# Attention and a mixture of experts in one kernel: when weights are split, on which engine, and how many output buffers

## The chip, the cores and the metric

The kernel runs on one core of a Trainium2 chip. The metric is the device time of one execution in microseconds (us), less is better. The engines are named as the profile names them: PE is TensorE's matmuls and PEld its weight loads, DVE is VectorE, ACT is ScalarE, POOL is GpSimd, SP is SyncE, whose queue here does nothing but start transfers. "Indirect" transfers, which gather or scatter rows by a table of indices, are started by POOL.

## The reference

```python
# attention: B, H, S, D = 4, 8, 768, 64; 4 sink tokens, window 128
scores = scale * q @ k.T
scores = where(is_sink | in_window, scores, -1e9)
a = softmax(scores);  attn = a @ v
# mixture of experts: x is 3072 x 512, E = 8 experts, F = 1024
x = attn.transpose(0, 2, 1, 3).reshape(3072, 512)
e_idx = argmax(x @ w_gate);  gate_w = softmax(x @ w_gate)[e_idx]
eom = sigmoid(x @ w_output_gate)
for e in range(8):
    h = maximum(x[e_idx == e] @ w1[e], 0)           # 512 -> 1024
    out[e_idx == e] = gate_w * eom[:, e] * (h @ w2[e])   # 1024 -> 512
```

## The kernel before

Attention runs in 16 steps up to about 196 us. Its rows go to `xd` in DRAM, and a router is worked out beside it: which token goes to which expert, and tables of indices (`final_table`, the last and longest part, runs on VectorE into the time of the experts; its lines are L398 to L446).

The experts' work is cut into **slots**, numbered by k from 0 to 16 (slot 16 runs only if its table has rows, and it has none in this profile). A slot is one expert with one to three blocks of up to 256 rows, or a "half" slot of one block of fewer rows (k = 5, 9 and 13). Slots 0 to 3 are the early ones (`NE` = 4), of experts that are known before all rows are. Each slot has two products: `first`, rows by w1 (the matmul of L561, L586 or L692), with ReLU behind it, and `second`, by w2 (L671, L596 or L708).

How a slot goes, engine by engine:

- **Rows.** `gather` (L514) starts an indirect transfer on POOL, `xg` from `xd`. TensorE transposes `xg` (L532), ScalarE casts the result to `xh` (L534), VectorE makes the rest, `xl` = x − `xh` (L535). The products of all slots but 0, 1 and the half ones are made of three terms, high × high, high × low and low × high.
- **Weights.** Each product takes four chunks of 512 KB. In half slots and slots 0 and 1 a chunk is loaded straight into its place. Elsewhere it goes into one of four `raw` buffers (`RAW` = 4, L491, on SP's queue); a **split** then casts it on ScalarE to its high half (L501) and subtracts that on VectorE or POOL to get the low half (L502): POOL for the chunks 0 and 2 of a product, VectorE for 1 and 3. The places of the chunks are named a0 to a3, b0 to b2, c0 to c5; `c3h` and `c3l` are the halves in place c3.
- **Between the products.** ScalarE makes `hh` from the first product (ReLU and cast, L541), VectorE the rest `hl` (L542).
- **Outputs.** `put` scales a result into `y` on ScalarE (L652), and POOL starts an indirect transfer of it into `out` (L653). Before the change `y` has two buffers. Transfers into `out` follow each other: each one waits on a semaphore of the one before.

Nothing is scheduled by the compiler: every engine runs its instructions in the order in which the program writes them. That order comes from a **planner** inside the kernel. It walks through TensorE's steps, adding up a nominal cost in `now` (`lane_step`); after each step `supply` may write the next chunk's split (`place`) into the order, if the chunk's place has been free for `LAG` units, its load was started `LAND` = 5 units ago, and the chunk before was placed at least `PACE` ago. `place` writes the split, which frees a raw buffer by its end, and `feed` starts the next raw load. At a product's beginning `ensure` writes all chunks of it that are still missing. A unit of `now` is meant as a microsecond of TensorE's work.

The lines that decide it, before:

```python
x = items[n_put[0]]
at = free.get(x["name"], 0)
if (x["again"] or at is not None and at <= now[0] - LAG) and now[0] >= put_at[0] + PACE:
    if x["split"] is None or x.get("at", now[0]) <= now[0] - LAND:
        place()
```

Of the kernel before, what the change touches and what calls it, by code (L numbers as in the profile page):

```python
# [7 lines left out]
F32 = mybir.dt.float32  # L8
F32R = mybir.dt.float32r
BF16 = mybir.dt.bfloat16  # L10
I32 = mybir.dt.int32
# [7 lines left out]
P = 128  # L19
# [4 lines left out]
DM = H * D  # L24
E, FF = 8, 1024
ND, NF = DM // P, FF // P
KW = T * (P + 4)
XW = DM + 1
# [6 lines left out]
NE = sum(n for _, n in ROUNDS)  # L35
# [6 lines left out]
HN = U * max(SIZES)  # L42
NJ = 16
JMAX = 27
NJP = NJ + 8
# [2 lines left out]
NB, RAW = 6, 4  # L48
JOINT = ((0,), (1,), (2,), (3,))
CW = P + 4  # L50
LAG, PACE, LAND = 0.7, 1.7, 5.0


def moe_kernel(tc, qT, kx, vx, vs, wgo, w1, w2, nsink, window, out):
# [5 lines left out]
    nc = tc.nc  # L60
    ctx = ExitStack()
    with ctx:
# [5 lines left out]
        mx = ctx.enter_context(tc.tile_pool(name="mx", bufs=2))  # L68
# [216 lines left out]
        def ids_of(tabv, shape, name):  # L285

            x1 = sm.tile(shape, F32, name=name + "_x")
            nc.vector.scalar_tensor_tensor(out=x1, in0=tabv[1], scalar=128.0, in1=tabv[0], op0=ALU.mult, op1=ALU.add)
            vd = sm.tile(shape, F32, name=name + "_v")
            ts(out=vd, in0=tabv[1], scalar1=0.0, scalar2=None, op0=ALU.is_gt)  # L290
            idm = sm.tile(shape, F32, name=name)
            nc.vector.scalar_tensor_tensor(out=idm, in0=x1, scalar=1.0 - P, in1=vd, op0=ALU.add, op1=ALU.mult)
            return idm
# [75 lines left out]
        def final_table(mp):  # L369
# [12 lines left out]
            yield "B"  # L382

            idm = ids_of((tab[:, 0], tab[:, 1]), [P, E, NJ], "idm")
            every = mp.tile([P, E, NJP, 4], I32, name="every", bufs=1)
            nc.vector.memset(every[:, :, NJ:NJP, 0:1], 0)
            for c, pad in ((1, NTOK), (2, 2 * NTOK), (3, 2 * NTOK)):
                nc.vector.memset(every[:, :, NJ:NJP, c:c + 1], pad)
# [2 lines left out]
            p = sm.tile([P, E, NJ], F32, name="pads_all", bufs=1)  # L391
# [7 lines left out]
            key = sm.tile([P, E], F32, name="key")  # L399
# [60 lines left out]
        w1v = w1.rearrange("e (d p) f -> e p d f", p=P)  # L460
        w2v = w2.rearrange("e (f p) d -> e p f d", p=P)

        def load_weights(which, ereg, slot, whole=False, parts=False):


            loads, splits = [], []
            src, k, n = ((w1v, ND, FF), (w2v, NF, DM))[which]
            his, los = [], []
            kk = k // 4
            for i in range(4):  # L470
                view = src[bass.ds(ereg, 1), :, i * kk:(i + 1) * kk, :].rearrange("o p k n -> p (o k) n")
                if whole:
                    if i % 2 == 0:
                        pool, name = slot()

                    def straight(pool=pool, name=name, i=i, view=view):
                        hi = (pool or pools[name[0]]).tile([P, kk, n], F32, name=name + "hl"[i % 2])
                        nc.sync.dma_start(out=hi, in_=view)
                        his.extend(hi[:, j, :] for j in range(kk))

                    if parts:
                        loads.append(straight)
                    else:
                        straight()
                    continue
                pool, name = slot()
                raws = []

                def load(view=view, raws=raws):
                    raws.append(stg.tile([P, kk, n], F32, name="raw"))  # L490
                    nc.sync.dma_start(out=raws[0], in_=view)  # L491

                def cast(pool=pool, name=name):
                    hi, lo = ((pool or pools[name[0]]).tile([P, kk, n], F32R, name=name + x) for x in "hl")
                    his.extend(hi[:, j, :] for j in range(kk))
                    los.extend(lo[:, j, :] for j in range(kk))
                    return hi, lo

                def split(raws=raws, cast=cast, eng=nc.vector if i % 2 else nc.gpsimd):
                    hi, lo = cast()  # L500
                    nc.scalar.copy(out=hi, in_=raws[0])  # L501
                    eng.tensor_tensor(out=lo, in0=raws[0], in1=hi.bitcast(F32), op=ALU.subtract)  # L502

                if parts:
                    loads.append(load)
                    splits.append(split)
                else:
                    load()
                    split()
            return ((his, los), loads, splits) if parts else (his, los)  # L510

        def gather(mp, ids, n=NTOK):
            xg = mp.tile([P, XW], F32, name="xg", bufs=3)
            nc.gpsimd.indirect_dma_start(out=xg, out_offset=None, in_=xd[0:n + 1, :],  # L514
                                         in_offset=bass.IndirectOffsetOnAxis(ap=ids[0], axis=0))
            return xg, mp.tile([P, 1], F32, name="sc", bufs=6)
# [131 lines left out]
            return hs  # L648

        def put(mp, ys, sc, m, where, rows, ids):  # L650
            y = mp.tile([P, DM], F32, name="y", bufs=2)[:, 0:m]
            nc.scalar.activation(out=y, in_=ys[:, 0:m], func=AF.Copy, scale=sc)  # L652
            nc.gpsimd.indirect_dma_start(out=where, out_offset=bass.IndirectOffsetOnAxis(ap=ids, axis=0),  # L653
                                         in_=y, in_offset=None, bounds_check=rows - 1, oob_is_err=False)
# [59 lines left out]
        def expert_reg(ap):  # L714
            return nc.sync.value_load(ap, min_val=0, max_val=E - 1)


        plan = [(order_i[0:1, r:r + 1], [(idx_e[:, 0, r, j:j + 1], idx_e[:, 1, r, j:j + 1]) for j in range(2)], False) for r in range(NE)]
# [4 lines left out]
        steps = []  # L723
# [26 lines left out]
        ws = {}  # L750
# [5 lines left out]
        def slot():  # L756
            name = next(order)
            return pools.get(name[0]), name

        with ExitStack() as actx:  # L760
# [220 lines left out]
            items, raws, names, free = [], [], {(0, 0): aa[:2], (0, 1): aa[2:], (1, 0): bb[:2], (1, 1): bb[2:] + aa[:1]}, {}  # L981
            for x in aa + bb:
                free[x] = None
            now, put_at, n_put, n_raw = [0.0], [0.0], [0], [0, 0]

            def build():
                if not todo or todo[0][0] >= NE and later:
                    return False
                k, w = todo.pop(0)
                if "e%d" % k not in ws:  # L990
                    ws["e%d" % k] = expert_reg(plan[k][0])
                used = names[k, w] = []

                def named():
                    pool, name = slot()
                    used.append(name)
                    return pool, name

                half = plan[k][2]
                ws[k, w], loads, splits = load_weights(w, ws["e%d" % k], named, half, True)  # L1000
                for i in range(4):
                    x = dict(key=(k, w), name=used[i // 2 if half else i], again=half and i % 2 == 1, load=loads[i],
                             split=None if half else splits[i])
                    items.append(x)
                    if not half:
                        raws.append(x)
                return True

            def feed():

                while n_raw[0] < n_raw[1] + RAW:
                    if n_raw[0] == len(raws):
                        if not build():
                            return
                        continue
                    x = raws[n_raw[0]]
                    x["load"]()
                    x["at"] = now[0]
                    n_raw[0] += 1

            def place():
                x = items[n_put[0]]
                n_put[0] += 1
                assert x["again"] or free.get(x["name"], 0) is not None
                free[x["name"]] = None
                if x["split"] is None:
                    x["load"]()
                else:
                    if "at" not in x:
                        feed()  # L1030
                    x["split"]()
                    n_raw[1] += 1
                    feed()
                put_at[0] = now[0]

            def supply():
                if n_put[0] == len(items) and not build():
                    return
                x = items[n_put[0]]
                at = free.get(x["name"], 0)  # L1040
                if (x["again"] or at is not None and at <= now[0] - LAG) and now[0] >= put_at[0] + PACE:
                    if x["split"] is None or x.get("at", now[0]) <= now[0] - LAND:
                        place()

            def ensure(key):
                while not all(x["key"] != key for x in items[n_put[0]:]) or key in todo:
# [224 lines left out]
            with tc.manual_schedule(engines={ET.PE, ET.Activation, ET.DVE, ET.Pool, ET.SP}):  # L1271
                for i in range(NP + 2):
                    if i == NP:
                        qctx.close()
                        mp = mctx.enter_context(tc.tile_pool(name="mp", bufs=2, side="right", reuse_waits="tile"))
# [196 lines left out]
```

## Time and profile before

| | |
|---|---|
| time before, median of 3 runs | 614.37 us (611.58 to 616.38) |
| the profiled execution's own time | 610.17 us |
| its span, first to last instruction | 608.4 us |
| mean granted TensorE clock | 0.952 of full |
| busy: PE, PEld | 521.0 us (86%), 393.6 us (65%) |
| busy: DVE, ACT, POOL | 325.5 us (54%), 269.0 us (44%), 302.4 us (50%) |
| DMA | 112.84 MB, 185 GB/s on average |

The profile describes one execution. Busy shares are averages over stages of quite different kinds, so the prediction looks at stretches of the span. In a row of the timeline the columns are the start and the length in us, the engine, the line, the operation, the output and inputs with their shapes, and, in brackets, how long the engine was idle just before and what ended that. A row ending in x4 groups four like instructions. The granted clock is the share of full speed at which TensorE was let run in a stretch; 0.50 is half speed. The last matmul ends at about 596 us; the last transfer into `out` takes the rest.

### The profile page before, as it was taken

To read this page: it belongs to the slowest core of one execution; us is meant where nothing else is said; L and a number is where in the kernel's file an instruction comes from. 1 tells how busy PE (TensorE), PEld (TensorE's weight loads), DVE (VectorE), ACT (ScalarE), POOL (GpSimd) and SP (SyncE) were. 2 spreads that over 40 slices of the span, in tenths; PEclk is the share of its full clock that TensorE was granted. 3 is DMA by queue.
4 is the path that set the end of the run, shared out by engine and by line. 5 is a ranking of instruction groups with operands and counts; after the bars stand their busy time and mean duration, and the time that the engine had idled before them with its cause. 6 is when DMAs were issued, how large, how long until landed. Compare 5 with 4: busy or idle time off the path is not lost. (4 is left out here: it accounts for less than half of the span.)

```text
span 608.4 us, 10491 instructions
## 1 busy us (share of the span) xinstructions
PE 521.0 (86%) x3432; PEld 393.6 (65%) x3432; DVE 325.5 (54%) x734; ACT 269.0 (44%) x721; POOL 302.4 (50%) x330
## 2 busy tenths in 40 slices
PE   3999999998799989399999989987999967958961
PEld 1566666665467638159989669866778757638740
DVE  5576798787686689942423642422335342342560
ACT  2577656666553225232633452433345451343420
POOL 4567667756763335424343755343347463353440
PEclk9999999999999999789999999998999987987976
DMA  6166865678987973454576666383836739464590
GB/s 217 59 154 176 188 124 134 191 139 183 265 144 218 203 216 107 149 164 141 172 260 224 226 229 210 122 272 120 296 114 209 242 126 343 156 236 148 143 378 22
DMA packets 72497, 112.84 MB, mean 185 GB/s; under 512 B 12044, under 2 KB 38672, under 8 KB 72434
## 3 DMA queue, kind: packets, MB, share of 16 engines
q1 hardware_dynamic: 67970, 98.16, 56.3%
q0 software_dynamic: 4464, 13.91, 6.3%
q8 instruction: 30, 0.49, 0.4%
q14 instruction: 33, 0.27, 0.1%
HBM read 98.28 MB, written 13.45 MB: 184 GB/s over the span
## 5 line engine op out<-in xcount | busy, mean ns | idle before, releaser
L831 ACT ACTIVATE e<-s,nmx 128x132 f32<-128x132 f32 x192 | 69.5, 367 | 66.5 <-DVE nmx L829 59.0
L819 PE MATMUL s<-kr,qr 64*128 64x260 f32 (+1 forms) x384 | 63.4, 431 | 17.1 <-ACT e L831 11.4
L542 DVE SCALAR_TENSOR_TENSOR hl<-s,hh 128x512 fp32r<-128x512 f32 (+1 forms) x32 | 24.2, 758 | 76.4 <-ACT hh L541 73.4
L819 PEld LDWEIGHTS s<-kr,qr 64*128 64x128 f32 x384 | 30.2, 198 | 41.3 <-ACT e L831 30.1
L541 ACT ACTIVATE hh<-s 128x512 fp32r<-128x512 f32 (+1 forms) x32 | 20.9, 652 | 75.2 <-PE s L561 70.8
L653 POOL DMA_INDIRECT out_dram<-y,idx x20 | 25.1, 1256 | 48.7 <-ACT y L652 23.0
L829 DVE TENSOR_REDUCE nmx<-s 128x2 f32<-128x264 f32 x96 | 41.5, 432 | 3.3
L806 POOL TENSOR_SCALAR qr<-qr 128x256 f32<-128x256 f32 x48 | 39.9, 851 | 1.6 <-DMA qr<-in_qT_dram 1.6
L535 DVE TENSOR_TENSOR xl<-tp,xh 128x512 fp32r<-128x512 f32 x21 | 14.4, 690 | 48.1 <-ACT xh L534 48.1
L84 POOL TENSOR_SCALAR_AFFINE_SELECT g<-f 128x512 f32<-128x512 f32 (+1 forms) x48 | 28.3, 590 | 21.0 <-DVE f L848 18.4
L831 ACT ACTIVATION_READ_ACCUMULATOR e<-s,nmx 128x1 f32 x192 | 37.7, 196 | 0.0
L825 DVE COPY_PREDICATED s<-maskf,s 128x256 f32<-128x256 int32 x80 | 33.7, 421 | 6.6 <-PE s L819 6.4
L532 PE MATMUL tp<-ident,xg 128*128 128x128 f32 x84 | 14.2, 296 | 20.9 <-DMA xg<-xd,idx_e 11.8
L534 ACT CAST xh<-tp 128x512 fp32r<-128x512 f32 x21 | 12.3, 587 | 41.2 <-PE tp L532 41.2
L842 PE MATMUL tp<-ident,e 128*128 128x128 f32 x192 | 29.3, 291 | 0.1
L842 PEld LDWEIGHTS tp<-ident,e 128*128 128x128 f32 x192 | 21.4, 146 | 11.4 <-issue 5.7
L84 POOL TENSOR_SCALAR_AFFINE_SELECT f<-f 128x512 f32<-128x512 f32 (+1 forms) x48 | 27.1, 564 | 3.3
L532 PEld LDWEIGHTS tp<-ident,xg 128*128 128x128 f32 x84 | 10.9, 151 | 25.8 <-DMA xg<-xd,idx_e 12.6
L514 POOL DMA_INDIRECT xg<-xd,idx x21 | 24.6, 1173 | 5.9 <-issue 4.0
L889 PE MATMUL oA<-f,vt 128*64 128x128 f32 x256 | 26.5, 285 | 0.4 <-DVE hl L871 0.2
L502 POOL TENSOR_TENSOR c0l<-raw,c0h 128x1024 fp32r<-128x1024 f32 x4 | 9.7, 2430 | 23.7 <-ACT c0h L501 23.7
L652 ACT ACTIVATE y<-oA,sc 128x512 f32<-128x512 f32 (+1 forms) x16 | 10.4, 650 | 23.4 <-DMA out_dram<-y,idx 9.3
(652 smaller groups left out, 1614.8 us busy)
## 6 DMA issues: line engine op xcount, KB each, us to landing
raw<-in_w_dram SPq DMA_DIRECT2D x88, 512.0 KB
kr<-in_kx_dram SPq DMA_DIRECT2D x16, 396.0 KB
qr<-in_qT_dram SPq DMA_DIRECT2D x16, 384.0 KB
vt<-in_vx_dram SPq DMA_DIRECT2D x16, 384.0 KB
xd<-x SPq DMA_DIRECT2D x16, 384.0 KB
a0h<-in_w_dram SPq DMA_DIRECT2D x4, 512.0 KB
a0l<-in_w_dram SPq DMA_DIRECT2D x4, 512.0 KB
b0h<-in_w_dram SPq DMA_DIRECT2D x3, 512.0 KB
```

The source lines that it names most:

```text
L84: nc.gpsimd.affine_select(out=ap, in_=ap if src is None else src, pattern=pattern, compare_op=op, fill=fill, base=base, channel_multiplier=cm)
L514: nc.gpsimd.indirect_dma_start(out=xg, out_offset=None, in_=xd[0:n + 1, :], in_offset=bass.IndirectOffsetOnAxis(ap=ids[0], axis=0))
L532: nc.tensor.transpose(out=tp[:, d, :], in_=xg[:, d * P:(d + 1) * P], identity=ident)
L542: nc.vector.scalar_tensor_tensor(out=lo, in0=ps, scalar=0.0, in1=hi.bitcast(F32), op0=ALU.max, op1=ALU.subtract)
L653: nc.gpsimd.indirect_dma_start(out=where, out_offset=bass.IndirectOffsetOnAxis(ap=ids, axis=0), in_=y, in_offset=None, bounds_check=rows - ...
L806: nc.gpsimd.tensor_scalar(out=q, in0=q, scalar1=SCALE, scalar2=None, op0=ALU.mult)
L819: nc.tensor.matmul(out=s[:, a, o0:P + CW], lhsT=z["q"][r, t * P:(t + 1) * P], rhs=z["k"][r, k0:k0 + P + CW - o0], start=True, stop=True)
L825: nc.vector.copy_predicated(out=both[:, :, 4:CW], mask=bc(maski[:, 1, 4:CW], 1, 2), data=s[:, :, 0:P])
L829: nc.vector.tensor_reduce(out=m, in_=both, axis=AX.X, op=ALU.max, negate=True)
L831: nc.scalar.activation(out=z["e"][:, t, a, :], in_=both[:, a, :], func=AF.Exp, bias=m[:, a:a + 1], scale=1.0, accum_out=z["rs"][:, t, a:a ...
L842: nc.tensor.transpose(out=tp[:, k, :], in_=z["e"][:, 2 * j + k // 2, k % 2, 4:CW], identity=ident)
L889: nc.tensor.matmul(out=o, lhsT=v[:, kt, r], rhs=src[:, kt, a, :], start=t == kt == 0 or t == kt + 1 == 4, stop=False, skip_group_check=True)
```

## The change

1. The pace at which splits are written is no longer 1.7 units throughout. The planner works out when each product begins (`due`, from 3.6 units for a half slot's product and 5.6 per block for others). A chunk whose product begins within 20 units (`SOON`) is placed 1.3 units after the last, one with more time 3.0 units after it.
2. The straight loads of half slots no longer count for the pace, and up to two places are looked at after each step.
3. From slot 4 on, POOL makes the low half of chunk 2 alone; VectorE makes the other three. Over the program 18 splits move from POOL (44 before, 26 now) to VectorE (44 before, 62 now).
4. `y` has four buffers (`YB`). To make room, a table of `final_table` (`every`) is put into the buffer that `xl` uses later.

```diff
-LAG, PACE, LAND = 0.7, 1.7, 5.0
+YB, XB = 4, 3
+LAG, PACE, SOON, LAND = 0.7, (3.0, 1.3), 20.0, 5.0
...
-            every = mp.tile([P, E, NJP, 4], I32, name="every", bufs=1)
+            every = mx.tile([P, ND, HN], F32R, name="xl", bufs=1).bitcast(I32).rearrange("p d c -> p (d c)")
+            every = every[:, 0:E * NJP * 4].rearrange("p (e j c) -> p e j c", e=E, j=NJP)
...
-                def split(raws=raws, cast=cast, eng=nc.vector if i % 2 else nc.gpsimd):
+                def split(raws=raws, cast=cast, eng=nc.gpsimd if i in onpool else nc.vector):
...
-            y = mp.tile([P, DM], F32, name="y", bufs=2)[:, 0:m]
+            y = mp.tile([P, DM], F32, name="y", bufs=YB)[:, 0:m]
...
+            due, t = {}, 4 * NF * 1.75
+            for f, k in steps + [("first", len(plan) - 1), ("second", len(plan) - 1)]:
+                due[k, 0 if f == "first" else 1] = t
+                t += 3.6 if plan[k][2] else 5.6 * len(plan[k][1])
...
-                ws[k, w], loads, splits = load_weights(w, ws["e%d" % k], named, half, True)
+                ws[k, w], loads, splits = load_weights(w, ws["e%d" % k], named, half, True, (0, 2) if k < NE else (2,))
...
-                put_at[0] = now[0]
 
             def supply():
-                if n_put[0] == len(items) and not build():
+                for _ in range(2):
+                    if n_put[0] == len(items) and not build():
+                        return
+                    x = items[n_put[0]]
+                    at = free.get(x["name"], 0)
+                    if not x["again"] and (at is None or at > now[0] - LAG):
+                        return
+                    if x["split"] is None:
+                        place()
+                        continue
+                    if now[0] >= put_at[0] + PACE[due[x["key"]] < now[0] + SOON] and x.get("at", now[0]) <= now[0] - LAND:
+                        place()
+                        put_at[0] = now[0]
                     return
```

TensorE's instructions stand in the same order before and after; those of ScalarE, VectorE, POOL and SP move. In the changed kernel the lines above are 1 to 14 further down (L502 is L504, L514 is L516, L535 is L537, L542 is L544, L653 is L655). Three places show the moves.

POOL between slots 1 and 2, before: the low halves of five chunks (a3 and c1, c3, c5 are slot 2's and 3's, b1 slot 3's), two stores of outputs, and the gathers of slot 2's rows.

```order
L653 DMA out_dram<-y,idx_e 3072x512 x2
L502 TENSOR_TENSOR a3l<-raw,a3h 128x1024
L502 TENSOR_TENSOR c1l<-raw,c1h 128x1024
L502 TENSOR_TENSOR c3l<-raw,c3h 128x1024
L502 TENSOR_TENSOR c5l<-raw,c5h 128x1024
L514 DMA xg<-xd,idx_e 128x513 x2
L502 TENSOR_TENSOR b1l<-raw,b1h 128x1024
```

And now:

```order
L655 DMA out_dram<-y,idx_e 3072x512 x2
L504 TENSOR_TENSOR a3l<-raw,a3h 128x1024
L504 TENSOR_TENSOR c1l<-raw,c1h 128x1024
L516 DMA xg<-xd,idx_e 128x513 x2
L504 TENSOR_TENSOR c3l<-raw,c3h 128x1024
L504 TENSOR_TENSOR c5l<-raw,c5h 128x1024
L655 DMA out_dram<-y,idx_e 3072x512 x2
```

The gathers moved ahead of c3l and c5l, which are placed later by the slower pace.

VectorE at the end of `final_table`, before (`nrem` and `more_i` are the table's last rows; c0l and c2l stand further up among its rows):

```order
L445 TENSOR_TENSOR nrem<-nrem,special 128x1
L446 CAST more_i<-nrem 128x1
L502 TENSOR_TENSOR c4l<-raw,c4h 128x1024
L502 TENSOR_TENSOR b0l<-raw,b0h 128x1024
L535 TENSOR_TENSOR xl<-tp,xh 128x4x128
L502 TENSOR_TENSOR b2l<-raw,b2h 128x1024
L535 TENSOR_TENSOR xl<-tp,xh 128x4x128
```

And now:

```order
L447 TENSOR_TENSOR nrem<-nrem,special 128x1
L448 CAST more_i<-nrem 128x1
L504 TENSOR_TENSOR c2l<-raw,c2h 128x1024
L504 TENSOR_TENSOR c4l<-raw,c4h 128x1024
L537 TENSOR_TENSOR xl<-tp,xh 128x4x128 x2
L504 TENSOR_TENSOR b0l<-raw,b0h 128x1024
```

c2l moved behind the table, b0l and b2l behind both of slot 2's `xl`.

POOL in the last slots (13 to 15), before: splits among stores and gathers.

```order
L653 DMA out_dram<-y,idx 3072x512 x2
L514 DMA xg<-xd,idx 128x513
L502 TENSOR_TENSOR c3l<-raw,c3h 128x1024
L653 DMA out_dram<-y,idx 6144x256
L502 TENSOR_TENSOR c5l<-raw,c5h 128x1024
L502 TENSOR_TENSOR b1l<-raw,b1h 128x1024
L502 TENSOR_TENSOR a0l<-raw,a0h 128x1024
L502 TENSOR_TENSOR a2l<-raw,a2h 128x1024
L502 TENSOR_TENSOR c0l<-raw,c0h 128x1024
L653 DMA out_dram<-y,idx 3072x512 x2
L514 DMA xg<-xd,idx 128x513
L502 TENSOR_TENSOR c2l<-raw,c2h 128x1024
```

And now:

```order
L504 TENSOR_TENSOR c5l<-raw,c5h 128x1024
L504 TENSOR_TENSOR a0l<-raw,a0h 128x1024
L655 DMA out_dram<-y,idx 3072x512 x2
L516 DMA xg<-xd,idx 128x513
L655 DMA out_dram<-y,idx 6144x256
L504 TENSOR_TENSOR c0l<-raw,c0h 128x1024
L504 TENSOR_TENSOR c4l<-raw,c4h 128x1024
L655 DMA out_dram<-y,idx 3072x512 x2
L516 DMA xg<-xd,idx 128x513
L655 DMA out_dram<-y,idx 3072x512
```

Between the pair of stores and the half slot's store (6144x256) no split is left.

More of the change, by code (lines that the diff above doesn't have):

```diff
@@ L461, in moe_kernel, with load_weights @@
         w2v = w2.rearrange("e (f p) d -> e p f d", p=P)
-        def load_weights(which, ereg, slot, whole=False, parts=False):
+        def load_weights(which, ereg, slot, whole=False, parts=False, onpool=(0, 2)):
             loads, splits = [], []
@@ L512, in gather @@
         def gather(mp, ids, n=NTOK):
-            xg = mp.tile([P, XW], F32, name="xg", bufs=3)
+            xg = mp.tile([P, XW], F32, name="xg", bufs=XB)
             nc.gpsimd.indirect_dma_start(out=xg, out_offset=None, in_=xd[0:n + 1, :],
@@ L1033, in place @@
                     feed()
-                put_at[0] = now[0]
             def supply():
-                if n_put[0] == len(items) and not build():
-                    return
[L1039 to L1043, printed above, removed]
+                for _ in range(2):
[11 more added lines that the diff above has]
+                        put_at[0] = now[0]
+                    return
             def ensure(key):
```

## The prediction

> **What bounds the kernel now.** I went from the stages to TensorE's waits in them, and from each wait to the engine named there. First the share of each engine in two stretches, the first slots and the last slots. The columns are the stretch, its length, the busy time of PE, PEld, DVE, ACT and POOL with instruction counts, the granted TensorE clock, and the DMA share with its GB/s.
>
> ```profile
> 260.00:340.00 80.00, 80.00 (x454) 66.61 (x455) 27.12 (x34) 32.64 (x50) 29.23 (x19) 0.98 0.61 199
> 500.00:596.00 96.00, 76.02 (x410) 60.94 (x408) 37.33 (x30) 33.79 (x50) 39.78 (x22) 0.88 0.64 224
> ```
>
> From 260 to 340 TensorE never rests; in the last 96 us it is idle for 20 and its clock falls to 0.88. No other engine is half full there, so it is order, not work, that holds TensorE up. TensorE's instructions stand in the same order before and after; the change can only move what TensorE waits for. These are its waits from 225 us on (total, times, longest):
>
> ```profile
> PE tp L532 <- DMA xg<-xd,idx_e: 11.8, 1, 11.8
> PE tp L532 <- DMA xg<-xd,idx: 9.1, 2, 5.5
> PE oA L671 <- POOL c2l L502: 5.8, 1, 5.8
> PE s L561 <- POOL c3l L502: 5.1, 1, 5.1
> PE s L561 <- POOL b0l L502: 3.9, 1, 3.9
> PE oA L708 <- ACT y L652: 3.4, 2, 2.6
> PE s L561 <- POOL c5l L502: 2.7, 1, 2.7
> ...
> PE s L561 <- DVE hl L542: 1.2, 1, 1.2
> ...
> PE s L561 <- DVE c5l L502: 0.5, 1, 0.5
> PE oA L708 <- DMA c2l<-in_w_dram: 0.2, 1, 0.2
> PE s L561 <- POOL c4l L502: 0.2, 1, 0.2
> ```
>
> The rows of weights (c2l, c3l, b0l, c5l twice, the load c2l, c4l) sum to 18.4 us, all after 499 us. A wait costs more than itself: the clock drops around it.
>
> ```profile
> 250.20:263.80 13.60, 3.87 (x8) 2.26 (x9) 12.84 (x33) 4.67 (x8) 7.54 (x4) 0.50 0.56 158
> 362.80:366.20 3.40, 3.40 (x20) 1.95 (x18) 1.39 (x1) 1.39 (x2) 2.58 (x2) 0.50 0.52 184
> 502.70:509.60 6.90, 4.20 (x19) 4.20 (x20) 0.45 (x1) 0.32 (x1) 4.56 (x4) 0.51 0.99 329
> 543.70:553.90 10.20, 6.16 (x27) 5.87 (x28) 2.43 (x2) 0.69 (x2) 5.46 (x3) 0.50 0.52 177
> 584.70:591.50 6.80, 4.42 (x12) 3.56 (x13) 6.16 (x2) 0.48 (x2) 4.64 (x2) 0.50 1.03 377
> ```
>
> Work done at half clock takes twice its time, so half of PE's busy time in such a stretch is lost: (4.20 + 6.16 + 4.42) / 2 = 7.4 us in the last three, which lie behind the waits for weights, 1.9 in the first and 1.7 in the second.
>
> **The weights' waits: −25.8.** Why a weight's low half comes late is seen on POOL (idle before, and its releaser, in brackets):
>
> ```profile
> 540.30 1.01 POOL L653 DMA_INDIRECT out_dram<-y,idx  x1 [3.61 <-ACT y L652]
> 542.63 2.35 POOL L502 TENSOR_TENSOR c3l<-raw,c3h 128x1024 fp32r<-128x1024 f32 x1
> 545.15 1.81 POOL L653 DMA_INDIRECT out_dram<-y,idx  x1 [0.17 <-issue]
> 546.97 2.37 POOL L502 TENSOR_TENSOR c5l<-raw,c5h 128x1024 fp32r<-128x1024 f32 x1
> ```
>
> c3l and c5l do not take long (2.4 us); c3l stands behind an output's store that idles POOL for 3.61 us, c5l behind c3l and a second store, and TensorE waits 5.1 and 2.7 us for them. The new planner puts these splits on the queues earlier. The old one placed the chunks of a late slot when the product began (the last of slot 12's second product at its beginning; likewise in 14 and 15); by the new numbers, slot 12's first product, due at planner time 249.6, has its four at 232.8 to 237, its second, due 264.4, at 245.4 to 249.6, slot 14's first (due 279.2) at 253.8 to 265.8, slot 15's second (due 307.2) at 287.6 to 294.6. A planner unit is near a microsecond of unhindered TensorE work, so the leads are 12 or more, against a longest delay of 5.8 in the rows above. Of the four late ones, three go to VectorE, which carries no stores. So I take all of it: 18.4 + 7.4 = 25.8. Bounds: 0 (the second rival) and 25.8, taken because a lead of 12 covers 5.8 twice.
>
> Eighteen splits change engine, at 2.4 us each on POOL (rows above) and 1.22 alone on VectorE (next fence): 43 us less on POOL, 22 more on VectorE, which is busy 37 of 96 in the last stretch. That costs nothing while VectorE has its gaps; without that cover, 22 us. The half slots' loads, now placed up to two at once on SP's queue, stand among raw loads; the only wait for such a load is the 0.2, counted already. The table `every` in `xl`'s buffer delays nothing: it is sent off at 226, and `xl` is first written at 263.27.
>
> **The gap at 248 to 260: −6.8.** Here TensorE has finished its early slots and waits for the rows of slot 2.
>
> ```profile
> 232.31 0.17 DVE L413 SCALAR_TENSOR_TENSOR over<-who,over 128x8 f32<-128x8 f32 x1
> 233.25 5.39 DVE L413 SCALAR_TENSOR_TENSOR over<-who,over 128x8 f32<-128x8 f32 x1
> 241.26 2.30 DVE L423 TENSOR_SCALAR prc<-prc 128x32 f32<-128x32 f32 x1
> 250.55 2.35 POOL L502 TENSOR_TENSOR c5l<-raw,c5h 128x1024 fp32r<-128x1024 f32 x1 [7.03 <-ACT c5h L501]
> 250.84 2.09 DVE L429 CAST lin_i<-osq 128x4 int32<-128x4 f32 x1
> 253.05 1.87 POOL L514 DMA_INDIRECT xg<-xd,idx_e  x1
> 257.58 2.50 DVE L441 TENSOR_TENSOR rem<-base,start 128x216 f32<-128x216 f32 x1
> 259.93 1.11 PE L532 MATMUL tp<-ident,xg 128*128 128x128 f32 x4 [11.80 <-DMA xg<-xd,idx_e]
> 260.99 1.22 DVE L502 TENSOR_TENSOR c4l<-raw,c4h 128x1024 fp32r<-128x1024 f32 x1
> 263.27 0.68 DVE L535 TENSOR_TENSOR xl<-tp,xh 128x512 fp32r<-128x512 f32 x1
> 270.94 0.68 PE L561 MATMUL s<-xh,a1h 128*128 128x256 f32 x1
> ```
>
> The gather at 253.05 stood behind c5l, whose cast waited for its raw load; in the changed order it stands right behind c1l, about 240 (c1h's cast is now a step later), and lands before 248. TensorE would go on at 248.1 (259.93 − 11.80) and be ready for slot 2 at 257.2 (its 11.0 us of work between 259.93 and 270.94, less 1.9 of half clock). But `xl` and c4l stand on VectorE behind the routing table, which runs there without a gap up to c4l at 260.99. From 233.25 the table has 27.7 us; 11.4 of them are the four long rows (5.39, 2.30, 2.09, 2.50), which took an estimated 0.9 in all without POOL's splits beside them, going by 0.17 for the first; c2l, a split like c4l's 1.22, stands among the table's rows and moves behind them. That leaves 15.1 of its own, to which I add four stalls for a3l, c1l, c3l and c5l: 3.0 and three of 2.3. The table then ends at 258.3, c2l and c4l at 260.7, two `xl` of 0.68 at 262.1. So slot 2 starts 8.8 us earlier than 270.94, less an estimated 2 for a clock halved again by TensorE's wait of 5 (1.9 and 1.7 above): −6.8. Bounds: 0 (VectorE ends the table where it did) and −13.7 (the wait of 11.8 and 1.9 all go); the value taken is their middle, because the stalls nearly keep their sum.
>
> **Four output buffers: −4.7.** ScalarE's y waited for a store to land before it could reuse a buffer, with hh behind it:
>
> ```profile
> 354.71 1.05 ACT L501 CAST c5h<-raw 128x1024 fp32r<-128x1024 f32 x1 [3.29 <-DMA raw<-in_w_dram]
> 361.03 0.70 ACT L652 ACTIVATE y<-oA,sc 128x512 f32<-128x512 f32 x1
> 368.39 0.47 ACT L652 ACTIVATE y<-oA,sc 128x256 f32<-128x256 f32 x1 [4.21 <-DMA out_dram<-y,idx]
> 458.96 0.47 ACT L652 ACTIVATE y<-oA,sc 128x256 f32<-128x256 f32 x1 [5.06 <-DMA out_dram<-y,idx]
> ```
>
> The second of these led to the wait of 1.2 for hl; with four buffers it goes. The 4.21 was beside TensorE's work and is worth nothing. The y at 361.03, for which TensorE waited 2.6, stood behind four casts, of which one waited 3.29 for its load; of this wait I take 1.8 plus 1.7 of clock, since the casts come earlier now but a cast may still be ahead. 1.2 + 3.5 = 4.7 (bounds 1.2 and 2.6 + 0.8 + 1.7 + 1.2 = 6.3).
>
> **What stays, and what comes new.** The two waits of 9.1 for later gathers stay: here is the first, and POOL's rows in that place are not moved.
>
> ```profile
> 406.63 0.98 POOL L653 DMA_INDIRECT out_dram<-y,idx  x1 [3.93 <-issue]
> 414.64 1.09 PE L532 MATMUL tp<-ident,xg 128*128 128x128 f32 x4 [5.51 <-DMA xg<-xd,idx]
> ```
>
> At the second (491 us) the y ahead of the stores now stands behind three casts in a run (c5h, b0h, b1h), each 1.05: I add 2 (bounds 0 and 5, a run that meets a late load). And more splits on VectorE mean more indirect transfers of POOL held up, as at 545.15 (1.81 against 1.01 alone): 0.8 each, of which I put one or two on TensorE's path: +1 (bounds 0, and 8 for ten of them).
>
> On this the Trainium skill speaks otherwise. Its page "SBUF — State Buffer", section "Who interferes with whom", infers that a `tensor_tensor` on VectorE leaves GpSimd's descriptor generation alone, since it takes only the read side of the port pair; by that the +1 would be 0. The 1.81 beside VectorE's split against 1.01 says that here it does not hold, so I keep my term.
>
> **Sum**, on the profiled execution's own time: 610.17 − 25.8 − 6.8 − 4.7 + 2 + 1 = 575.9. The timed median, 614.37, lies 4.2 above that execution; carried over, about 580.
>
> **Rivals.** *The raw buffers run dry* (0.12). The new pace places splits 1.3 to 1.4 apart in six bursts of four to seven; four raw buffers are refilled by 512 KB loads, and at 354.71 ScalarE waited 3.29 for one and TensorE 2.6 + 1.7 of clock soon after. If every burst did that: 6 × 4.3 = 26 more, 606; if half of them, 593. Against it: the chunk is placed no sooner than five units after its load was issued, and DMA is busy 0.6 of the time.
>
> *The change does not do what it says* (0.07). The splits left on POOL (c5l, a0l, c0l, c4l late on) still stand among stores, and POOL idles up to 3.93 at one (406.63). If the weights' 25.8 and the table's 6.8 stay: 575.9 + 32.6 + 4.2 = 613. Against it: they are placed 12 units ahead.
>
> *VectorE becomes the bound* (0.05), the slower side. hl comes behind splits on VectorE's queue, and one split beside POOL's took this:
>
> ```profile
> 344.18 6.34 DVE L502 TENSOR_TENSOR c2l<-raw,c2h 128x1024 fp32r<-128x1024 f32 x1 [2.31 <-ACT c2h L501]
> ```
>
> Where three of four splits are on VectorE, such a row ahead of an hl makes it late by 6.34 − 2.8, the length of one block of TensorE's first product: 3.5, and 1.7 of clock. From the fifth slot on nine slots with splits are left (the other three are half slots, whose weights are not split): once in each is 47, or 575.9 + 47 + 4.2 = 627. It decides from seven of the nine on, where 7 × 5.2 eats the gain of 34. Against it: such a long row needs two POOL splits back to back, and POOL's fall from 44 to 26. The Trainium skill has this rule on the same page and section: two inputs in SBUF on VectorE contend with GpSimd's reads, and the first to issue shuts the other out for its whole length. The 6.34 agrees with it; it does not say how often the two will meet.
>
> **How the numbers follow.** A measurement of this kernel can tell about 1% from no change, 608 to 621. Forecast, 567 to 592, 0.70; below 567 (the whole 13.7 at the table goes and nothing new comes) 0.06; raw buffers, 592 to 607, 0.12; no effect 0.07; VectorE 0.05. Faster: 0.70 + 0.06 + 0.12 = 0.88; same 0.07; slower 0.05. The range, 567 to 603, takes in most of the raw buffers' case.
>
> **What would show it.** The waits for c2l, c3l, b0l and c5l gone from TensorE's list after 499 us, and its clock there above 0.95; the table's last row on VectorE near 258 and a first product of slot 2 near 262; no y that waits for out_dram; the gathers' 9.1 still there. I am wrong if ScalarE's casts show waits for raw of over 2 us right ahead of TensorE's gaps, or hl heads TensorE's list.

## The result, and the profile after

| | before | changed |
|---|---|---|
| median beside each other | 612.98 us (610.97 to 616.38) | 580.75 us (578.93 to 583.63) |
| ratio, 95% interval | | 0.947 (0.941 to 0.954) |
| the profiled execution's own time, span | 610.17, 608.4 us | 580.31, 578.5 us |

The change makes the kernel 5.3% faster. First the two stretches shown before, in the changed kernel (its last one ends earlier); the columns are the same.

```profile
260.00:340.00 80.00, 77.23 (x465) 67.52 (x464) 37.04 (x36) 36.26 (x53) 32.94 (x22) 1.00 0.75 249
...
500.00:566.00 66.00, 60.57 (x348) 48.74 (x347) 24.96 (x28) 25.52 (x39) 19.18 (x13) 0.97 0.69 236
```

In the last slots TensorE is busy 60.6 of 66 us where it was 76 of 96, at a clock of 0.97 instead of 0.88. Its waits from 225 us on are these, all of them:

```profile
PE tp L534 <- DMA xg<-xd,idx: 14.9, 2, 8.9
PE tp L684 <- DMA xg<-xd,idx: 5.6, 3, 3.6
PE s L621 <- DVE hr L602: 3.0, 3, 1.5
PE s L563 <- DVE xl L537: 1.6, 1, 1.6
PE oA L710 <- ACT y L654: 1.6, 2, 0.8
PE tp L608 <- DVE hr L602: 0.3, 1, 0.3
```

No weight stands in the list any more, no hl, and not the 11.8 us for slot 2's rows. What has grown are the waits for gathered rows: two of 14.9 in full slots (9.1 before) and three in half slots (L684). The stretches of half clock moved with them:

```profile
222.35:225.75 3.40, 3.40 (x7) 1.48 (x5) 2.89 (x10) 0.00 (x0) 0.00 (x0) 0.50 0.31 93
399.85:406.65 6.80, 4.86 (x17) 4.09 (x18) 1.45 (x3) 1.89 (x5) 0.00 (x0) 0.50 0.14 57
478.35:488.60 10.25, 3.89 (x14) 3.33 (x15) 0.93 (x2) 1.15 (x3) 1.59 (x2) 0.50 0.56 210
505.65:509.05 3.40, 3.40 (x17) 3.40 (x17) 0.00 (x0) 0.29 (x1) 0.00 (x0) 0.50 1.04 395
```

Three of the four stand at the three waits for gathers at 402, 485 and 505 us.

Since TensorE's order is the same, the start of one and the same matmul can be compared in the two traces. The differences show where the time went (starts of the same instruction, in us; the lead is changed less before, so a minus means that the changed kernel is ahead, and the step is what the lead gained or lost since the row above):

| instruction in both | before | changed | lead | step |
|---|---|---|---|---|
| slot 0's first matmul, at attention's end | 200.24 | 201.40 | +1.2 | |
| slot 1, `oB` with a3h | 222.55 | 225.04 | +2.5 | +1.3, half clock at 222 |
| slot 2, first product, second matmul | 271.46 | 262.20 | −9.3 | −11.8, the gap at the table |
| half slot 5, second product | 365.58 | 352.59 | −13.0 | −4.0 at the wait for y, +0.3 ahead of it |
| rows of half slot 9 | 430.89 | 419.97 | −10.9 | +2.1, gathers |
| slot 10, first product | 462.28 | 450.03 | −12.3 | −1.3, hl |
| slot 11, first product | 483.34 | 471.61 | −11.7 | +0.5 |
| slot 11, second product begun | 492.47 | 487.08 | −5.4 | **+6.3, gather of slot 12** |
| slot 12, first product | 509.41 | 495.86 | −13.6 | −8.2, weights |
| half slot 13's rows, just behind | 517.46 | 508.89 | −8.6 | **+5.0, gather of the half slot** |
| slot 14, first product | 553.40 | 533.95 | −19.5 | −10.8, weights (−0.1 ahead of them) |
| slot 15, second product | 591.08 | 563.60 | −27.5 | −7.6, weights (−0.5 ahead of them) |
| own time | 610.17 | 580.31 | −29.9 | −2.4, behind the last matmul |

### The profile page after: what moved, and what is told of

It is laid out like the page before. It is cut to its first block, busy times and chain, and to the rows that moved or that the text cites. A ratio compares the mean times of both kernels' runs of the same rounds, so it can differ in the third digit from the quotient of the medians.

```text
span 578.5 us, 10477 instructions
## 1 busy us (share of the span) xinstructions
PE 513.3 (89%) x3432; PEld 390.0 (67%) x3432; DVE 330.5 (57%) x752; ACT 269.5 (47%) x721; POOL 257.9 (45%) x312
## 5 line engine op out<-in xcount | busy, mean ns | idle before, releaser
L821 PE MATMUL s<-kr,qr 64*128 64x260 f32 (+1 forms) x384 | 63.1, 430 | 16.2 <-ACT e L833 10.8
L544 DVE SCALAR_TENSOR_TENSOR hl<-s,hh 128x512 fp32r<-128x512 f32 (+1 forms) x32 | 24.2, 757 | 58.2 <-ACT hh L543 52.8
L655 POOL DMA_INDIRECT out_dram<-y,idx x20 | 24.4, 1219 | 59.1 <-DMA idx<-unitd 14.5
L537 DVE TENSOR_TENSOR xl<-tp,xh 128x512 fp32r<-128x512 f32 x21 | 14.4, 689 | 45.0 <-ACT xh L536 45.0
L536 ACT CAST xh<-tp 128x512 fp32r<-128x512 f32 x21 | 12.3, 587 | 35.8 <-PE tp L534 35.8
L655 POOL DMA_INDIRECT out_dram<-y,idx_e x8 | 10.0, 1254 | 39.0 <-ACT y L654 22.3
L534 PE MATMUL tp<-ident,xg 128*128 128x128 f32 x84 | 13.8, 291 | 14.9 <-DMA xg<-xd,idx 14.9
L516 POOL DMA_INDIRECT xg<-xd,idx x21 | 22.1, 1051 | 10.8 <-issue 5.5
L891 PE MATMUL oA<-f,vt 128*64 128x128 f32 x256 | 26.5, 285 | 0.4
L848 ACT COPY f<-tp 128x512 f32<-128x512 f32 x32 | 18.6, 582 | 0.4 <-PE tp L844 0.4
```

Source lines behind the costliest of these rows:

```text
L534: nc.tensor.transpose(out=tp[:, d, :], in_=xg[:, d * P:(d + 1) * P], identity=ident)
L544: nc.vector.scalar_tensor_tensor(out=lo, in0=ps, scalar=0.0, in1=hi.bitcast(F32), op0=ALU.max, op1=ALU.subtract)
L821: nc.tensor.matmul(out=s[:, a, o0:P + CW], lhsT=z["q"][r, t * P:(t + 1) * P], rhs=z["k"][r, k0:k0 + P + CW - o0], start=True, stop=True)
L891: nc.tensor.matmul(out=o, lhsT=v[:, kt, r], rhs=src[:, kt, a, :], start=t == kt == 0 or t == kt + 1 == 4, stop=False, skip_group_check=True)
```

## The experiments

Twelve runs, three sessions of four; each ratio is to the kernel before in the same session. One thing must be known for reading single profiles: slot 0's first matmul, at 200.24 us before, starts between 197.5 and 206.5 in the fourteen profiles, with TensorE's instructions in the same order up to there. So a profile's span says little about differences of 1%; the ratios and the rows from 200 us on do.

**Each part alone.** Engines alone, on the kernel before:

```diff
-        def load_weights(which, ereg, slot, whole=False, parts=False):
+        def load_weights(which, ereg, slot, whole=False, parts=False, onpool=(0, 2)):
...
-                def split(raws=raws, cast=cast, eng=nc.vector if i % 2 else nc.gpsimd):
+                def split(raws=raws, cast=cast, eng=nc.gpsimd if i in onpool else nc.vector):
...
-                ws[k, w], loads, splits = load_weights(w, ws["e%d" % k], named, half, True)
+                ws[k, w], loads, splits = load_weights(w, ws["e%d" % k], named, half, True, (0, 2) if k < NE else (2,))
```

> The kernel before with one edit: from slot 4 on POOL makes only the low half of chunk 2, VectorE the other three; times of the splits and buffers as before. Theory (the splits were placed too late, and POOL's stores only made it worse): the last slots' chunks are still written at their product's beginning, so about half of the 18.4 us of waits for weights and of the 7.4 of clock stays, now named to VectorE; the gap of 11.8 at slot 2 is unchanged. About 600 us (595 to 606). Rival (POOL as such was the cause): all waits for weights go, 587 to 590. Second rival (VectorE becomes the bound): hl late, 615 or more.

Measured: 0.976 (0.969 to 0.983), 595.3 us. The median fits the theory at its lower edge, but the way there does not. TensorE's waits for weights in this kernel:

```profile
PE s L561 <- POOL c5l L502: 7.2, 1, 7.2
PE s L561 <- POOL b0l L502: 3.9, 1, 3.9
...
PE oA L671 <- POOL c4l L502: 1.6, 1, 1.6
...
PE s L561 <- ACT b0h L501: 0.8, 1, 0.8
PE s L561 <- ACT c5h L501: 0.8, 1, 0.8
...
PE oA L671 <- DVE c3l L502: 0.3, 1, 0.3
```

14.6 of the 18.4 us stay, 12.7 of them named to POOL (I had expected VectorE there): the one split in four that is left on it stands behind the stores as before. The waits for c3l and c2l (5.1 and 5.8), whose splits went to VectorE, are gone, but TensorE then meets the next chunk that is still on POOL: it goes on with c5l at 539.67 instead of 549.39 and has waited 7.2 us for it instead of 2.7, and it waits 1.6 for c4l, for which it had not waited in that place. So moving splits to VectorE moves most of the waits from one chunk to the next. Half of them were to go; only a fifth went. A kernel with the old times and no late split on POOL at all was not run.

The profile is 14.4 us shorter than that of before. 2.8 of it lie ahead of slot 0, which is chance; 3.3 are the wait for y at 361 with its clock, 4.4 lie between 496 us and the last matmul, 2.2 behind the last matmul, and the rest is in small pieces.

Times alone (the changed kernel with the old engines and two buffers):

```diff
-YB, XB = 4, 3
+YB, XB = 2, 3
...
-                ws[k, w], loads, splits = load_weights(w, ws["e%d" % k], named, half, True, (0, 2) if k < NE else (2,))
+                ws[k, w], loads, splits = load_weights(w, ws["e%d" % k], named, half, True, (0, 2))
```

> The changed kernel with the splits' engines as before (POOL for chunks 0 and 2 in all slots) and two y buffers: only the times of placing are new. Theory: the waits for weights go to under 4 us although POOL still makes half of the splits, and the first product of slot 2 begins near 260 as in the changed kernel; the waits for y (2.6 and 1.2) stay in part. 583 to 592 us. Rival (the engine matters): 10 us or more of waits for low halves on POOL stay, 597 to 606.

Measured: 0.964 (0.958 to 0.971), 588.3 us. TensorE's longest waits:

```profile
PE tp L534 <- DMA xg<-xd,idx: 14.8, 2, 8.6
PE tp L684 <- DMA xg<-xd,idx: 7.1, 3, 3.8
PE s L563 <- DVE hl L544: 5.3, 4, 2.2
PE s L563 <- DVE xl L537: 3.7, 1, 3.7
```

No wait for a weight, with half of the splits still on POOL. That is the theory's case: the weights were late because they were placed late. New are 5.3 us for hl in four places. In two of them (2.6 us) hl stands behind a split of VectorE that took 3.2 us beside one of POOL's; in the other two (2.8 us) the hh ahead of hl stands behind a y that waited for a store, 7.0 and 5.3 us, as there are two buffers here.

Buffers alone, on the kernel before:

```diff
-            every = mp.tile([P, E, NJP, 4], I32, name="every", bufs=1)
+            every = mx.tile([P, ND, HN], F32R, name="xl", bufs=1).bitcast(I32).rearrange("p d c -> p (d c)")
+            every = every[:, 0:E * NJP * 4].rearrange("p (e j c) -> p e j c", e=E, j=NJP)
...
-            y = mp.tile([P, DM], F32, name="y", bufs=2)[:, 0:m]
+            y = mp.tile([P, DM], F32, name="y", bufs=4)[:, 0:m]
```

> The kernel before with four y buffers (and the table `every` in the buffer of xl, which makes room). Theory: the y that waited for a store at 459 and its hl go, and the y at 361 is not helped, since it stood behind casts that waited for loads: 1 to 3 us faster, 611 to 613. Rival (the stores' landing holds TensorE up at 361 too): 5 to 6 faster, 608 to 609. If it is slower, y's earlier end starts transfers that collide with gathers.

Measured: 1.000 (0.997 to 1.003). No y waits for a store any more and the wait for hl at 462 is gone, but that is worth nothing that can be measured, and the wait for y at 361 stays:

```profile
PE oA L709 <- ACT y L653: 3.3, 2, 2.5
```

In this profile TensorE also waited only 4.9 us for slot 2's rows (11.8 before), and its lead over before was 5.4 us at slot 10, of which 3.1 were left at the end. The timed runs show nothing of it; whether the buffers or chance shortened that wait was not tried.

**Buffers and engines, taken out of the changed kernel.** Two y buffers:

```diff
-YB, XB = 4, 3
+YB, XB = 2, 3
```

> The changed kernel with two y buffers instead of four; everything else as changed. Theory (a y that waits for a store to land holds hh and the casts behind it, and the outputs now come closer together): 2 to 6 us slower than the changed kernel, 583 to 587. Rival (the buffers do nothing here either, as on the kernel before): 579 to 582.

Measured: 0.952 (0.944 to 0.960), 583.7 us. The same kernel was run again beside the changed one, in five rounds:

> The changed kernel once more, as the measure for the three beside it: 0.947 of before (0.941 to 0.954), 576 to 584 us.

> The changed kernel with two y buffers, in the same session as the changed kernel. Theory (ScalarE's 14 us of waits for stores lie beside TensorE's work for the most part): 0 to 4 us slower than the changed kernel, too little to name a loss of more than 1%. Rival (the buffers are a needed part of the change): 5 us slower or more.

Measured: the changed kernel 0.949 (0.945 to 0.954), 581.1 us; with two buffers 0.957 (0.952 to 0.962), 583.7 us. Some 0.8%, 2.6 us between the medians, with intervals that overlap: between nothing and 1.5%. That fits the lower end of the first expectation; the buffers are a small part of the change at most.

The old engines in the changed kernel:

```diff
-                ws[k, w], loads, splits = load_weights(w, ws["e%d" % k], named, half, True, (0, 2) if k < NE else (2,))
+                ws[k, w], loads, splits = load_weights(w, ws["e%d" % k], named, half, True, (0, 2))
```

> The changed kernel with the low halves shared as before (POOL for chunks 0 and 2 in all slots); new times and four y buffers. Theory (with half of the splits on POOL, VectorE's splits and hl are shut out more often, while the waits for the weights themselves stay away): 4 to 8 us slower than the changed kernel, 584 to 589, with waits for hl of 4 us or more on TensorE's list. Rival (once the splits are early, the engine does not matter): 579 to 582.

Measured: 0.964 (0.954 to 0.975), 591.7 us. That is 9 to 11 us above the changed kernel (0.947 and 0.949, from other sessions, with intervals that touch). With two y buffers the same change of engines, from 0.964 of times alone to 0.952 and 0.957, is worth 4 to 8 us. So the old engines cost something between 4 and 11 us; the sign I had for it is missing: the hl waits sum to 1.6 us, not 4. Of the 9.9 us by which this profile is longer than the changed kernel's, 2.2 lie ahead of slot 0, 2.2 behind the last matmul, and the rest is spread over small waits and a half clock at slot 2. And no split on POOL from slot 4 on:

```diff
-                ws[k, w], loads, splits = load_weights(w, ws["e%d" % k], named, half, True, (0, 2) if k < NE else (2,))
+                ws[k, w], loads, splits = load_weights(w, ws["e%d" % k], named, half, True, (0, 2) if k < NE else ())
```

> The changed kernel with no split on POOL from slot 4 on: VectorE makes all four low halves of each product. Two of four on POOL took about 10 us more than one of four. Theory (what the second split on POOL cost is VectorE shut out by it, so the last one on POOL costs too): 2 to 6 us faster than the changed kernel. Rival (VectorE becomes the bound, hl waits behind its splits): 5 us or more slower, with hl heading TensorE's list. Third: POOL's gathers and stores are held up by VectorE's splits, so that the waits for xg grow: same to 4 slower.

Measured: 0.944 (0.939 to 0.949), 578.9 us, beside 0.949 for one in four: 2 to 3 us by these figures, but the intervals overlap, so a gain is not shown. VectorE does not become the bound even with all four. What that does to the splits is read from their own rows between 262 and 600 us (busy time of VectorE's and of POOL's splits with counts, then clock and DMA), in this order: before, the old engines in the changed kernel, the changed kernel, none on POOL.

```profile
262.00:600.00 338.00, 76.17 (x41) 91.67 (x38) 0.94 0.60 203
```
```profile
262.00:600.00 338.00, 73.25 (x42) 97.86 (x39) 0.95 0.62 207
```
```profile
262.00:600.00 338.00, 83.81 (x58) 52.00 (x21) 0.95 0.61 206
```
```profile
262.00:600.00 338.00, 94.96 (x78) 7.25 (x3) 0.95 0.62 207
```

One VectorE split takes 1.86, 1.74, 1.44 and 1.22 us on average: the fewer POOL makes, the shorter is one of VectorE's. Seventeen more splits cost VectorE only 7.6 us more (83.8 against 76.2), and POOL 40 less. The Trainium skill ("SBUF — State Buffer", "Who interferes with whom") says that VectorE with two SBUF inputs contends with GpSimd's reads; these means agree with it.

**The gap at the table alone**, on the kernel before:

```diff
-                if (x["again"] or at is not None and at <= now[0] - LAG) and now[0] >= put_at[0] + PACE:
+                if (x["again"] or at is not None and at <= now[0] - LAG) and now[0] >= put_at[0] + (3.0 if now[0] < 50.0 else PACE):
```

> The kernel before with one edit: splits are placed 3.0 units apart while the planner's time is under 50 (up to slot 2's first product), 1.7 after as before. POOL and VectorE then stand around the routing table's end as in the changed kernel. Theory (the gap at slot 2 is worth 9 us by itself, and nothing of the later waits for weights changes): 7 to 11 us faster than before, slot 2's first product at or near 261. Rival (the later waits absorb it, since the splits follow the planner and not TensorE): 0 to 4 faster.

Measured: 0.986 (0.977 to 0.995), 604.8 us: about 9 us. In its profile slot 2's second matmul begins at 262.92 (271.46 before), the lead over before stays between 6.6 and 9.1 us to the end, and the later waits for weights are all still there. So the two gains, at the table and in the late slots, are separate; this run gives the first by the times alone, and times alone gave both.

**Gathers ahead of the stores.** What remains in the changed kernel are the waits for gathers. I moved the gathers of the next slot's rows in front of the product's stores, in the changed kernel and in the kernel before (the same edit):

```diff
-                    if f == "first" and len(xgs[k]) == 1:
-                        rest = parts
-                    else:
-                        assert next(parts, None) is None
                     if x is not None:
                         assert next(x, None) is None
                         queue.pop(0)
                         rows_of(queue[0])
+                    if f == "first" and len(xgs[k]) == 1:
+                        rest = parts
+                    else:
+                        assert next(parts, None) is None
```

> The changed kernel, but the gathers of the next slot's rows are written ahead of the last product's stores instead of behind them. Theory (the gathers come late because the second store waits for the first to land, 4 to 5 us each on POOL): of the 20.5 us of TensorE's waits for xg in slots and half slots 15 or more go, and some 5 of clock with them: 558 to 566 us. Rival (the gather is late for its indices or its landing of 5 us, whatever stands ahead): 576 to 581. Rival (a gather that waits for its buffer now holds up the stores and splits behind it): 581 to 590.

Measured: 0.915 (0.908 to 0.922), 557.5 us, 20 to 24 us better than the changed kernel (by the ratios and by the medians, from two sessions) and just past the theory's range. POOL at slot 12's gathers in this kernel, then all of TensorE's waits:

```profile
459.19 1.86 POOL L516 DMA_INDIRECT xg<-xd,idx  x1 [0.16 <-issue]
461.36 0.97 POOL L516 DMA_INDIRECT xg<-xd,idx  x1 [0.30 <-issue]
462.64 1.02 POOL L655 DMA_INDIRECT out_dram<-y,idx  x1 [0.30 <-issue]
468.54 1.00 POOL L655 DMA_INDIRECT out_dram<-y,idx  x1 [4.87 <-ACT hh L629]
```
```profile
PE s L621 <- DVE hr L602: 2.9, 3, 1.3
PE s L563 <- DVE xl L537: 2.5, 1, 2.5
PE tp L684 <- DMA xg<-xd,idx: 2.3, 2, 1.3
PE oA L710 <- ACT y L654: 1.6, 2, 0.8
PE tp L608 <- DVE hr L602: 0.3, 1, 0.3
PE tp L534 <- DMA xg<-xd,idx: 0.2, 1, 0.2
```

20.5 us of waits for gathers became 2.5. The second store still idles POOL for 4.87 us, but slot 12's gathers no longer stand behind it. The gather of the half slot after it does (474.67), and TensorE waits 1.0 us for that one.

> The kernel before with one edit: the gathers of the next slot's rows are written ahead of the last product's stores. Theory (the waits of 5.5 and 3.6 us for xg at 414 and 491, and about 3 us of half clock behind them, come from the stores ahead): 9 to 13 us faster than before; since the waits for weights stay, no more. Rival (the splits in front of a late slot stand behind the gathers, which now wait for their buffers, and come later still): same or slower.

Measured: 0.980 (0.970 to 0.991), 604.1 us, 10 to 12 us as the theory had it. On the changed kernel the same edit is worth about twice as much, and its waits for gathers are about twice as long (20.5 us against 9.1).

> Both edits on the changed kernel: gathers ahead of the stores, and no split on POOL from slot 4 on. If both hold and add: 550 to 557 us. If the gathers ahead already hid POOL's share: 556 to 560, the same as with the gathers alone. If VectorE becomes the bound now that TensorE waits for nothing else: 562 or more.

This kernel has both edits, whose diffs stand above. Measured: 0.911 (0.905 to 0.916), 557.0 us: the second of the three cases, no more than the gathers ahead give alone. Against the 578.9 of none on POOL in the same session, the gathers ahead are worth 22 us. The two kernels with the gathers ahead are the fastest versions here.

## Why the prediction was right, point by point

**The total.** Predicted 580, measured 580.75. On the profiled executions I had −34.3 and they show −29.9; the changed kernel's profile lies 0.4 below its median where that of before lay 4.2 below, which made up for the difference. So 580 was close by the cancelling of two errors of 4 us.

**The weights, −25.8: −26.5** (8.2, 10.8 and 7.6 in the table). Mechanism and size hold. In the changed kernel's trace the low halves that were late are done long ahead: c3l 32 us before TensorE uses it, b0l 24, c2l 18, c5l 16, where I had 12 or more. One reading was wrong: of the four late ones two go to VectorE (c3l and c2l), not three; b0l and c5l stay on POOL. The sum does not change by it, as times alone, with all four made where they were, remove all waits for weights; engines alone take away a fifth.

**The gap at the table, −6.8: −9.3 by the clock, −11.8 from the last common point.** The rows follow the working closely:

```profile
236.26 2.90 DVE L413 TENSOR_SCALAR who<-key,top 128x8 f32<-128x8 f32 x1
240.99 2.03 DVE L431 CAST lin_i<-osq 128x4 int32<-128x4 f32 x1
243.14 1.00 POOL L516 DMA_INDIRECT xg<-xd,idx_e  x1
247.61 2.36 DVE L420 TENSOR_TENSOR prc<-who,io 128x32 f32<-128x32 f32 x1
253.16 2.35 DVE L427 TENSOR_TENSOR prc<-prc,io8n 128x8 f32<-128x8 f32 x1
258.48 0.15 DVE L448 CAST more_i<-nrem 128x1 int32<-128x1 f32 x1
259.89 0.68 PE L563 MATMUL s<-xh,a1h 128*128 128x256 f32 x1
260.87 1.28 DVE L537 TENSOR_TENSOR xl<-tp,xh 128x512 fp32r<-128x512 f32 x2
262.20 0.38 PE L563 MATMUL s<-xl,a1h 128*128 128x256 f32 x1 [1.63 <-DVE xl L537]
```

Four stalls, the table done at 258.6 (258.3 worked out), `xl` at 262.2 (262.1). The step that failed is the 2 us taken off for the clock: TensorE reached slot 2 at 259.89 and waited 1.63, not 5, so its clock did not fall. It came later by the half clock at 222 and by attention's end, and lost nothing by that, as `xl` was the last to come either way.

**Four output buffers, −4.7: −5.3 at these two places, but 4.0 of it not from the buffers.** Buffers alone gave 1.000; they remove the 1.3 for hl, and that is too little to be measured. The wait at 361 shrank from 2.6 to 0.1 with the new times: y now stands ahead of b0h and b1h on ScalarE. In times-only and in engines-only, both with two buffers, 0.8 is the longest wait for a y that is left. In engines-only the order of the casts is the old one, but c4h, c5h and b0h, ahead of y, no longer wait for their loads (2.9, 3.3 and 1.7 us before). I had put the buffers' name on a gain that belonged to the casts ahead of y, which my own sentence gave as the cause.

**The gather at 491, +2: +6.3, outside its bound of 5.** The first fence has POOL's stores and the first gather in the kernel before, the second the same place in the changed kernel, with ScalarE's and SP's rows ahead of POOL's.

```profile
481.22 1.00 POOL L653 DMA_INDIRECT out_dram<-y,idx  x1
486.51 0.98 POOL L653 DMA_INDIRECT out_dram<-y,idx  x1 [4.28 <-DMA out_dram<-y,idx]
487.80 0.99 POOL L514 DMA_INDIRECT xg<-xd,idx  x1 [0.30 <-issue]
```
```profile
468.53 1.05 ACT L503 CAST b1h<-raw 128x1024 fp32r<-128x1024 f32 x1 [1.14 <-DMA raw<-in_w_dram]
469.48 0.68 ACT L654 ACTIVATE y<-oA,sc 128x512 f32<-128x512 f32 x1
...
474.48 0.45 SPq L480 DMA_DIRECT2D b2h<-in_w_dram  x1
476.29 0.33 SPq L480 DMA_DIRECT2D a0l<-in_w_dram  x1
...
476.69 0.98 POOL L655 DMA_INDIRECT out_dram<-y,idx  x1 [4.86 <-DMA out_dram<-y,idx]
477.98 0.99 POOL L516 DMA_INDIRECT xg<-xd,idx  x1 [0.30 <-issue]
```

TensorE stood still from 487.57 before (491.20 − 3.63) and from 475.84 now (484.71 − 8.87). The first gather started 0.2 us after that before, 2.1 us after it now: this is the 2 that I had, y behind b0h and b1h. The rest is the landing: 3.4 us before, 6.7 now. In that time the transfers of four half-slot chunks (2 MB, started between 474.48 and 476.29) and raw loads were under way. I had counted these loads at nothing; the change places them earlier and without pace. The DMA engines were busy 0.92 of the time while the longer landing lasted and 0.63 in the shorter one. Other gathers of the two traces go the same way: 3.3 to 3.6 us at a share of 0.54 to 0.64 (before, at 282, 488 and 542), 7.2 to 7.5 at 0.98 to 1.00 (before at 507; changed at 319, 500 and 501); in between they scatter (3.9 us at 0.29 and at 0.87). That these loads lengthened the landing is likely from this, but was not tried apart. The half clock behind the longer wait took 1.1 more.

**What the prediction left out.** The gathers of half slots, 5.6 us where there were none (+5.0 at 505 alone, with its clock): they stand behind stores in the same way. I had looked only at waits that existed; with TensorE faster, gathers that had slack lost it. In gathers_first 3.3 of the 5.6 go, so most of it was the stores ahead.

**+1 for held-up indirect transfers** cannot be told apart: they are there (the store at 527.40 took 1.81 in the changed kernel), but none of TensorE's waits is named to one. The reading behind the term, that a split on VectorE holds such a transfer up, holds in all traces: from 200 us on, of 207 indirect transfers that POOL began while a split of VectorE ran, 186 took more than 1.1 us, up to 2.04; of the 558 others none took more than 1.06.

**The rivals.** *Raw buffers:* ScalarE's waits for raw sum to about 12 us after and 25 before, and none stands right ahead of a TensorE gap except the 1.14 above. *No effect* fell. *VectorE the bound:* hl is not on TensorE's list, and VectorE's splits grew by 7.6 us over these slots, not by my 22, since each took less time. With all splits on VectorE it still is not the bound.

## What to carry to other kernels

Where an engine waits for a prepared operand, look first at when its preparation is written into the queues, and only then at the engine that makes it: here the times were worth 22 us alone, the engines' share 4 to 11 in the changed kernel (15 on the kernel before, so the two overlap) and buffers nothing that can be measured. When the longest waits go, ask what had slack only because of them; those that come next (here gathers behind stores) are found in the same order of rows, and moving them was worth another 20 to 24 us. On an in-order queue put what the critical engine needs ahead of what only has to be done sometime.

## What the runs showed of the hardware that was not expected

- The granted clock halved for 3.4 us at about 222 us in the changed kernel and in nine more of the fourteen profiles, and not in the other four, that of before among them, at the same two gaps of 1.4 and 1.1 us behind each other. The Trainium skill ("TensorE: Matmul & The Clock Gate", "What's actually happening") says that the window in which activity is counted is free-running and does not start with the kernel. If so, the same gaps can fall differently into it from one execution to the next; the profiles agree with that, without proving it.
- From the end of TensorE's last matmul (595.2 us before) to the end of the span it took 13.1 to 13.3 us in every profile with two of four late splits on POOL or with none; with one of four it took 11.0, in engines-only too. The 2 us lie at one place, a semaphore instruction of POOL (L1427 before, L1441 in the changed kernel): it ends 0.5 us after the branch ahead of it where the tail is 11.0, and 2.5 to 2.7 us after it elsewhere. This is most of the −2.4 of the table's last row; what it waits for is open.
